# V in eight aligned blocks with key windows copied by DMA, a merged table multiply and a split last row block, in an attention and state space kernel

## The chip, the cores and the metric

The kernel runs on one core of a Trainium2 chip. The metric is the device time of one execution in microseconds (us), and the time before is the median of 11 runs. The core has TensorE (PE, matrix products into PSUM), VectorE (DVE), ScalarE (ACT), GpSimd (POOL) and SyncE (SP), which here issues nearly all transfers. They run side by side and meet through semaphores. PSUM is used as four units of two banks; a bank holds 512 float32 columns.

## The reference, cut to what matters

Two heads of work on inputs of 2048 positions and 448 features, side by side in the output. The first is attention in 16 heads of 28 over 8 keys at distances 0, 2, ..., 14. The second is a complex diagonal recurrence (state space) with real input and output.

```python
# A: sliding dilated attention
qkv = (x @ wqkv).reshape(B, S, 3, H, Dh)          # S=2048, H=16, Dh=28
idx = pos[:, None] - arange(8) * 2                # keys of a query
logits = einsum("bhsd,bhswd->bhsw", q, kg) * Dh ** -0.5   # masked where idx < 0
a = einsum("bhsw,bhswd->bhsd", softmax(logits), vg) @ wo
# B: state space
Bu = x @ B_bar.T                                  # complex, 448 states
h = Lam_bar * h + Bu[:, t]                        # for t in 0..2047
y = 2 * (hseq @ Cmat.T).real + x * Dskip
out = concatenate([a, y], -1)
```

## The kernel before, in words

Even and odd positions stand side by side, so that 2048 positions become 1024 pairs; keys at even distances are then neighbours. x comes in transposed by DMA (`xA` for attention, `xB` for the recurrence).

Attention goes over nine query blocks b. A block has 112 query pairs (the first 128) and 128 key pairs, from `k0(b)` = 112b on; neighbouring key blocks overlap by 16. V is made for each of the nine key blocks: `v{b}` on TensorE (14 matmuls in pairs of row halves, through `pair`, with a handshake by GpSimd, `tick`, in the middle), `ev{b}` evicts it to `Vt`. Each head has 29 columns there, the last one a one (`g_one`), which makes the sum of the softmax. Q and K come in column chunks 0 to 256, 256 to 512 and 512 to 1024 (`q0`, `q1`, `q2` in RANK). Their weights are spread out into `Wpad` in four quarters (`wp`), each by ScalarE or VectorE. For block b and parity: scores `s` (mask product L702, key product L706), exponentials `x` on ScalarE (L712) into one of three buffers `Pb`, the product with V `a{b}` (32 matmuls, L724), the division `n{b}` on VectorE (L730, L731), and a transposing DMA `ot{b}` into `OT`. Last, `w{t}` multiplies by `wo`.

The recurrence works in two halves of 512 pairs and four state groups k, of which k = 3 is half as large. `b` is the input product (L764, with `WT`, which seven transposing DMAs `wtx` make from `l1`, `l2`), `be` its eviction to `u`. VectorE then rotates by a table of cosines and sines (`ma`: L777, L778 or L780, L781; `ri`: L788, L789), scans (`sc`, L798), and rotates back (`mb`, then `ro`, L806, L807) into h. The table is made by `t0`, `tk`, `ts`, `t2`, `t3`, `t4` on ScalarE and VectorE. C comes in by transposing DMAs (`ctl`), and `cg`, `ch` make the scaled matrices C1 and C2 of it on VectorE (L841) after ScalarE or VectorE has scaled one part (`wtmp`). `g` makes `Gm` from C1. For each of eight row blocks t, `y{t}` is the even part (L962 with C2, L964 with Gm) and `z{t}` the odd part (L971 with C1, L974 and L976 with a diagonal for the skip, which for t = 4 to 6 VectorE adds from `xd` instead). Row block 7 evicts its odd part in two halves of 224 columns, one on ScalarE and one on VectorE, and stores it in one DMA.

The order on each engine is not the order in the source. Each step is a node with a cost, dependencies and a rank (`RANK`: start and slope over the index of a group). `Plan.run` walks a clock for each engine and takes the ready node of lowest rank; evictions that free a PSUM unit go first, and the emitted order follows. On the chip each engine runs its list in order, whatever the clock of the plan said. Rings limit how far things run ahead: `mm` four PSUM units, `P` three, `O` three, `u` three, `wt` two, `ab`, `rv`, `rs` one.

```python
n0, n1 = halves(f"v{b}", 0.188, pe, [vw], ("v", b), h, at_x(k0(b) + 128))
vn[b] = node(f"ev{b}", ab(2 * D), ev, [n1], ("v", b), frees=[(n0, 0)])
n3 = node(f"a{b}", {"P": 0.93}, pv, xs + [vn[b]] + g_1 + g_z, ("a", b), alloc="mm", frees=[(xs[0], 0), (xs[2], 0)])
```

Of the kernel before, what the change touches and what calls it, by code (L numbers as in the profile page):

```python
# [16 lines left out]
NB = 9  # L17
# [8 lines left out]

RANK = {"v": (-247.7, 33.131), "q0": (-32.25, 20.848), "q1": (-1351, 261.899), "s": (-328.09, 66.43), "a": (312.95, 100.698), "b0": (348.52, -7.748),
        "b1": (2537.88, -155.645), "d0": (308.87, 213.856), "d1": (1776.4, -98.058), "l": (1991.99, 151.071), "t": (810.76, -33.643), "tk": (305.69, 160.366),
        "xd": (2014.82, -97.299), "cg": (910.27, 8.203), "ch": (1106.04, 1.621), "g": (869.44, 168.173), "y": (701.29, 136.506), "w": (1120.33, 1.167),
        "gu": (1198.03, -204.258), "q2": (787.17, -9.125), "wp": (320.49, 73.04)}  # L30

# [185 lines left out]
def kernel(  # L217
# [24 lines left out]
    def t_(shape, dt, name, tag=None):  # L242
        return sb.tile(shape, dt, tag=tag or name, name=name)
# [16 lines left out]
    Qt = t_([128, 4, 2, NP], BF16, "Qt")  # L260
    Vt = t_([128, 2, NB, H, 29], BF16, "Vt")
    Pb = [t_([128, 4, 4, 128], BF16, f"P{i}") for i in range(3)]
# [26 lines left out]
    ACT.dma_start(Wraw[0:64, 3, :], A_wqkv[384:448, 0:2 * D])  # L289
    for i, vec in ((0, B_log_dt), (2, B_Lambda_im), (3, B_Dskip)):  # L290
        G.dma_start(rows[7 * i:7 * i + 7, :], vec.rearrange("(c p) -> c p", p=64))
    for i in range(1, 4):
        xbar_x(xA, xA2, 128 * i, 128 * i + 128)
    ACT.dma_start(rows[7:14, :], B_Lambda_re.rearrange("(c p) -> c p", p=64))
    ACT.dma_start(Wraw[:, 0:3, D:2 * D], wmain(1))
# [10 lines left out]
    SP.dma_start(Pt[64:128, :], B_B_re[384:448, :])  # L306
    xbar_x(xB, xB2, 0, 256)
    xbar_x(xB, xB2, 256, 512)

# [33 lines left out]
    def g_one(e, a):  # L343
        G.memset(Vt[:, a, :, :, 28:29].rearrange("p b h o -> p (b h) o"), 1.0)

# [194 lines left out]

    plan = Plan({"mm": 4, "P": 3, "O": 3, "wt": 2, "u": 3, "rv": 1, "rs": 1, "ab": 1})
    lazy = {}
# [107 lines left out]
    vn = {}  # L650
    for b in range(NB):
        h = {}

        def pe(part, b=b, h=h):
            if part == 0:
                h["ps"] = unit()
            pair(h, part, h["ps"], D, lambda o, k: xA[o:o + 64, k, k0(b):k0(b) + 128], lambda o, k: Wv[o:o + 64, k, :])

        def ev(e, b=b, h=h):
            evac(e, Vt[:, :, b, :, 0:28], h["ps"][:, :, 0:D].rearrange("p a (h d) -> p a h d", h=H))  # L660
        n0, n1 = halves(f"v{b}", 0.188, pe, [vw], ("v", b), h, at_x(k0(b) + 128))
        vn[b] = node(f"ev{b}", ab(2 * D), ev, [n1], ("v", b), frees=[(n0, 0)])
    qn = {}
    CH = ((0, 256), (256, 512), (512, 1024))
# [22 lines left out]
    for b in range(NB):  # L687
# [32 lines left out]
        def pv(e, b=b, h=h, hb_=hb_):  # L720
            av = h["av"] = unit()
            for par in range(2):
                for hd in range(H):
                    PE.matmul(av[:, par, 29 * hd:29 * hd + 29], hb_[par]["P"][:, hd // 4, hd % 4, :], Vt[:, par, b, hd, :], start=True, stop=True)  # L724

        def nm(e, b=b, n=n, h=h):
# [5 lines left out]
                            rc.unsqueeze(3).to_broadcast((n, 2, H, DH)), ALU.mult)  # L732
        n3 = node(f"a{b}", {"P": 0.93}, pv, xs + [vn[b]] + g_1 + g_z, ("a", b), alloc="mm", frees=[(xs[0], 0), (xs[2], 0)])
        n4 = node(f"n{b}", {"V": 1.42}, nm, [n3, g_r], ("a", b), alloc="O", frees=[(n3, 0)])
# [19 lines left out]
    for hf in range(2):  # L754
        for k in range(4):
# [15 lines left out]
            def mul(e, src, k=k, h=h, big=big):  # L771
                c, s = tab[:, 0, k, :], tab[:, 1, k, :]
                a = h["a"] = wk.tile([128, 2, HALF], BF16, tag="ra", name="ra", bufs=1)
                x = h[src]
                if big:
                    b = h["b"] = wk.tile([128, 2, HALF], BF16, tag="rb", name="rb", bufs=1)
                    V.tensor_tensor(a[:], x[:], c.unsqueeze(1).to_broadcast((128, 2, HALF)), ALU.mult)  # L777
                    V.tensor_tensor(b[:], x[:], s.unsqueeze(1).to_broadcast((128, 2, HALF)), ALU.mult)  # L778
                else:
                    V.tensor_tensor(a[:, 0], x[:, 0], c, ALU.mult)  # L780
                    V.tensor_tensor(a[:, 1], x[:, 0], s, ALU.mult)  # L781

            def ri(e, k=k, h=h, big=big):
                a = h["a"]
                v = h["v"] = wk.tile([128, 2, HALF], BF16, tag="rv", name="rv", bufs=1)
                if big:
                    b = h["b"]
                    V.tensor_tensor(v[:, 0], a[:, 0], b[:, 1], ALU.add)  # L788
                    V.tensor_tensor(v[:, 1], a[:, 1], b[:, 0], ALU.subtract)  # L789
                else:  # L790
                    V.tensor_tensor(v[0:64, 0], a[0:64, 0], a[64:128, 1], ALU.add)
                    V.tensor_tensor(v[64:128, 0], a[64:128, 0], a[0:64, 1], ALU.subtract)

# [7 lines left out]
            def ro(e, k=k, hf=hf, h=h, big=big):  # L801
                hb, a = hbuf(hf), h["a"]
                to = slice(1, HALF + 1)
                if big:
                    b = h["b"]
                    V.tensor_tensor(hb[:, k, to], a[:, 0], b[:, 1], ALU.subtract)  # L806
                    V.tensor_tensor(hb[:, k + 4, to], a[:, 1], b[:, 0], ALU.add)  # L807
                    if hf == 0:
                        V.tensor_copy(ini[:, k:k + 5:4], hb[:, k:k + 5:4, HALF])
                else:  # L810
                    V.tensor_tensor(hb[0:64, 3, to], a[0:64, 0], a[64:128, 1], ALU.subtract)
                    V.tensor_tensor(hb[64:128, 3, to], a[64:128, 0], a[0:64, 1], ALU.add)
                    if hf == 0:
                        V.tensor_copy(ini[:, 3:4], hb[:, 3, HALF:HALF + 1])
# [3 lines left out]
            n2 = node(f"be{hf}{k}", ab(1024 if big else 512), ev, [n1], rb_, alloc="u", frees=[(n1, 0)])  # L818
            m1_ = node(f"ma{hf}{k}", {"V": 1.25 if big else 0.8}, lambda e, mul=mul: mul(e, "u"), [n2, t4], rd_(0), alloc="ab", frees=[(n2, 0)])
            x = ri_ = node(f"ri{hf}{k}", {"V": 0.75 if big else 0.86}, ri, [m1_], rd_(-0.1), alloc="rv", frees=[(m1_, 0)])  # L820
            for i in range(2 if big else 1):
                x = node(f"sc{hf}{k}{i}", {"V": 1.18}, lambda e, i=i, sc=sc: sc(e, i), [x] + ([rout[0, k]] if hf else []), rd_(-0.2),
                         alloc="rs" if i == 0 else None, frees=[(ri_, 0)] if i == (1 if big else 0) else [])
                if i == 0:
                    s0 = x
            m2_ = node(f"mb{hf}{k}", {"V": 1.25 if big else 0.8}, lambda e, mul=mul: mul(e, "s"), [x, t4], rd_(-0.3), alloc="ab", frees=[(s0, 0)])
            free_ = list(wp.values()) if hf == 0 else qdone + vdone + [rout[0, j] for j in range(4)]
# [123 lines left out]
    for t in range(8):  # L951
# [14 lines left out]
        def pe1(e, t=t, tk=tk, h=h, hf=hf):  # L966
            if t == 7:
                h[1] = unit()
            ps, hb, lo = h[1], hbuf(hf), 128 * (t % 4)
            for m in range(7):  # L970
                PE.matmul(ps[:, 1, 0:D], hb[:, m, lo + 1:lo + 129], lazy["C1"][:, m, :], start=(m == 0), stop=(t in YD and m == 6), skip_group_check=True)  # L971
            if t in YD:
                return
            PE.matmul(ps[:, 1, 0:64], xB[:, 3, tk], dgO[:, 0, 0:64], start=False, stop=False, skip_group_check=True)  # L974
            for k in range(3):
                PE.matmul(ps[:, 1, 64 + 128 * k:192 + 128 * k], xB[:, 4 + k, tk], dgO[:, 1 + k, :], start=False, stop=(k == 2), skip_group_check=True)  # L976

        def ev(e, a, b, h=h):
# [8 lines left out]
        n0 = node(f"y{t}", {"P": 2.0}, pe0, hs + c2 + gn + (wdone if t > 4 else []), r, alloc="mm")  # L987
        n1 = node(f"z{t}", {"P": 1.35 if t in YD else 1.57}, pe1, [n0] + c1, (r[0], r[1], -0.1), alloc="mm" if t == 7 else None)
        if t == 7:
            g2["deps"].append(n1)  # L990
        if t < YD[0]:
# [8 lines left out]
        else:  # L1000
            def half(e, lo, hi, h=h):
                evac(e, h["o"][:, 1, lo:hi], h[1][:, 1, lo:hi])
            n2 = node(f"ye{t}0", ab(D), lambda e, ev=ev: ev(e, 0, 1), [n0] + qdone, r, frees=[(n0, 0)])
            node(f"yo{t}0", {"S": 0.6}, lambda e, st=st: st(e, 0, 1), [n2], 60 + 3 * t, lat=2.2)
            n3 = [node(f"ye{t}{1 + i}", {"AV"[i]: 0.3}, lambda e, i=i, half=half: half(e, 224 * i, 224 * i + 224), [n1, n2], r, frees=[(n1, 0)])
                  for i in range(2)]
            node(f"yo{t}1", {"S": 0.5}, lambda e, st=st: st(e, 1, 2), n3, 61 + 3 * t, lat=2.2)

# [39 lines left out]
```

## Time and profile before

| what | value |
|---|---|
| median of 11 runs | 137.59 us |
| lowest, highest | 137.15, 140.05 us |
| the profiled execution | 137.28 us, of which the span is 135.6 |
| TensorE busy | 127.9 us, 94% of the span |
| VectorE busy | 109.8 us, 81% |
| ScalarE busy | 89.7 us, 66% |
| GpSimd busy | 29.0 us, 21% |
| V products, L528 and L529 | 63 matmuls each, about 350 ns each, in pairs |
| rotations, 1024 columns (L777, L778) | 24 operations, 682 to 690 ns |
| DMA | 15.59 MB, mean 115 GB/s |

The profile is of one execution. The span runs from the first to the last recorded event; the execution's own time is a little longer. Busy times overlap, so their sum is no time. Matmuls are pipelined: one is longer in the record than the step from its start to the next one's, so steps are read from starts. Idle time in a row is that of its engine just before it, with what ended it. The line numbers L are those of the kernel before.

### The profile page before, as it was taken

The numbers are of one execution on the slowest core, as the hardware profiler recorded it, in microseconds if no ns is written. First come the engines' busy times: TensorE is split into PE (matmuls) and PEld (weight loads), VectorE is DVE, ScalarE is ACT, GpSimd is POOL, SyncE is SP. The second block draws the span as 40 slices with busy tenths as digits, with TensorE's granted clock in tenths as the row PEclk, the third lists the DMA queues.
The fourth block names the chain that finished last, engine by engine and source line by source line (L and its number), as shares of the span: only waits on it lengthen the run. The fifth ranks groups of instructions, "written<-read, shape, count | busy, mean of one in ns | idle before, by whom it ended". The sixth has DMA issues, their size and how long they took to land.

```text
span 135.6 us, 3784 instructions
## 1 busy us (share of the span) xinstructions
PE 127.9 (94%) x1525; PEld 70.0 (52%) x1530; DVE 109.8 (81%) x204; ACT 89.7 (66%) x122; POOL 29.0 (21%) x110
## 2 busy tenths in 40 slices
PE   6989999999989999999999999999999999999980
PEld 2334757787434554564544465654665655455540
DVE  0438999999989899999999999999999999911110
ACT  0039999979995966999967998754875237511120
POOL 6985154013899500000000000000000000000000
PEclk9999999999999999999999999999999999999999
DMA  3999998509679587133020008741134788442121
GB/s 90 249 323 247 261 196 149 73 2 111 119 150 194 115 169 140 35 64 59 0 45 19 0 0 64 181 120 68 63 71 118 169 88 277 151 135 73 68 102 44
DMA packets 42755, 15.59 MB, mean 115 GB/s; under 512 B 34927, under 2 KB 42735, under 8 KB 42735
## 3 DMA queue, kind: packets, MB, share of 16 engines
q1 hardware_dynamic: 41264, 14.11, 49.7%
q10 hardware_dynamic: 1374, 1.21, 3.0%
q8 instruction: 13, 0.21, 0.7%
q14 instruction: 8, 0.06, 0.2%
q0 software_dynamic: 96, 0.00, 0.1%
HBM read 3.62 MB, written 3.67 MB: 54 GB/s over the span
## 4 chain that ended last, share of the span: by engine, by line
PE 74%; ACT 15%; POOL 5%; issue 2%; DVE 0%; POOLq 0%; ACTq 0%
PE mm L528 22%; PE mm L764 14%; PE mm L962 8%; PE mm L971 8%; PE mm L724 6%; PE mm L964 4%; PE mm L861 4%; PE mm L702 4%; PE mm L706 3%; ACT Wpad L501 2%; ACT Wpad L500 2%; POOL mst L312 2%; ACT tab L454 1%; ACT P L712 1%; ACT Wpad L497 1%
## 5 line engine op out<-in xcount | busy, mean ns | idle before, releaser
L712 ACT ACTIVATE P<-mm 128x896 bf16<-128x896 f32 (+1 forms) x36 | 31.5, 933 | 4.9 <-PE mm L706 4.9
L528 PE MATMUL mm<-xA,Wpad 64*128 64x256 bf16 (+1 forms) x168 | 27.0, 305 | 0.3 <-DVE Qt L507 0.3
L529 PE MATMUL mm<-xA,Wpad 64*128 64x256 bf16 (+1 forms) x168 | 26.8, 305 | 0.1
L505 ACT CAST ys<-mm 128x896 bf16<-128x896 f32 (+2 forms) x15 | 11.4, 771 | 19.1 <-PE mm L971 8.9
L536 POOL MEMSET tick<- 1x1 f32 x41 | 4.9, 119 | 84.9 <-PE mm L529 84.7
L764 PE MATMUL mm<-xB,WT 128*128 128x512 bf16 x93 | 22.2, 379 | 0.6 <-ACT P L712 0.3
L528 PEld LDWEIGHTS <-Wpad 64*128 64x128 bf16 x168 | 15.0, 94 | 7.4 <-POOL tick L536 0.6
L529 PEld LDWEIGHTS <-Wpad 64*128 64x128 bf16 x168 | 14.8, 94 | 1.6 <-issue 0.8
L764 PEld LDWEIGHTS <-WT 128*128 128x128 bf16 x98 | 9.0, 98 | 11.2 <-issue 1.1
L528 PE MATMUL mm<-Wv,xA 64*128 64x448 bf16 x63 | 13.7, 349 | 1.1 <-POOL tick L536 0.6
L529 PE MATMUL mm<-Wv,xA 64*128 64x448 bf16 x63 | 13.7, 350 | 0.0
L971 PE MATMUL mm<-C,h 128*128 128x448 bf16 x56 | 11.9, 353 | 0.0
L962 PE MATMUL mm<-C,h 128*128 128x448 bf16 x56 | 11.9, 353 | 0.0
L528 PE MATMUL mm<-wo,OT 64*128 64x448 bf16 x56 | 10.8, 349 | 0.0
L529 PE MATMUL mm<-wo,OT 64*128 64x448 bf16 x56 | 10.8, 349 | 0.0
L731 DVE TENSOR_TENSOR O<-mm,rcs 112x896 bf16<-112x896 f32 (+1 forms) x9 | 9.8, 1091 | 0.3
L528 PEld LDWEIGHTS <-xA 64*128 64x128 bf16 x63 | 5.5, 94 | 6.5 <-POOL tick L536 1.8
L996 DVE TENSOR_TENSOR ys<-mm,xd 128x448 bf16<-128x448 f32 x3 | 1.9, 625 | 8.5 <-ACT ys L505 8.5
L507 DVE CAST Vt<-mm 128x896 bf16<-128x896 f32 x6 | 6.4, 1086 | 2.9 <-PE mm L529 2.9
L724 PE MATMUL mm<-Vt,P 128*128 128x29 bf16 x288 | 8.7, 176 | 0.0
L798 DVE TENSOR_TENSOR_SCAN rs<-p_r,ini,rv 128x512 bf16<-128x512 f32 x7 | 8.6, 1270 | 0.0
L798 DVE TENSOR_TENSOR_SCAN rs<-p_r,rv 128x512 bf16<-128x512 f32 x7 | 8.5, 1221 | 0.0
(175 smaller groups left out, 247.3 us busy)
## 6 DMA issues: line engine op xcount, KB each, us to landing
out_dram<-ys SPq DMA_DIRECT2D x15, 224.0 KB, 2.4
Wraw<-in_A_wqkv_dram ACTq DMA_DIRECT2D x2, 336.0 KB, 4.0
wo<-in_A_wo_dram SPq DMA_DIRECT2D x2, 336.0 KB, 3.3
Wv<-in_A_wqkv_dram ACTq DMA_DIRECT2D x1, 336.0 KB, 3.5
natW<-in_B_B_re_dram SPq DMA_DIRECT2D x1, 336.0 KB
natW<-in_B_B_im_dram SPq DMA_DIRECT2D x1, 336.0 KB, 5.0
xo<-in_B_x_dram SPq DMA_DIRECT2D x1, 336.0 KB
out_dram<-ys SPq DMA_DIRECT2D x2, 112.0 KB, 1.7
```

Of the source, the lines that this page charges most:

```text
L505: ACT.copy(o, i)
L507: V.tensor_copy(o, i)
L528: x = PE.matmul(ps[:, a, 0:n], lhs(0, lo[i]), rhs(0, lo[i]), start=(i == 0), stop=(i == 6), skip_group_check=True)
L529: y = PE.matmul(ps[:, b, 0:n], lhs(64, hi[i]), rhs(64, hi[i]), start=(i == 0), stop=(i == 6), skip_group_check=True)
L702: PE.matmul(at(g)[:, 0:4 * n].rearrange("p (s q) -> p s q", s=4), msk[32 * g:32 * g + 32, 0, :], msk[32 * g:32 * g + 32, 1:2, c0:c0 + n].t ...
L712: ACT.activation(P[:].rearrange("p s g q -> p g s q")[:, 2 * z:2 * z + 2, :, 0:n], h["s"][z][:, :, 0:4 * n].rearrange("p g (s q) -> p g s ...
L724: PE.matmul(av[:, par, 29 * hd:29 * hd + 29], hb_[par]["P"][:, hd // 4, hd % 4, :], Vt[:, par, b, hd, :], start=True, stop=True)
L731: V.tensor_tensor(O[0:n, :].rearrange("p (a h d) -> p a h d", a=2, h=H), avv[0:n, :, :, 0:DH], rc.unsqueeze(3).to_broadcast((n, 2, H, DH)) ...
L764: PE.matmul(ps[:, i, :], WT[:, j, 128 * m:128 * m + 128], xB[:, j, HALF * hf:HALF * hf + HALF], start=(j == 0), stop=(j == 6))
L798: V.tensor_tensor_scan(h["s"][:, i], p["r2"][:, k:k + 1].to_broadcast((128, HALF)), h["v"][:, i], 0.0 if hf == 0 else ini[:, m:m + 1], ALU ...
L962: PE.matmul(ps[:, 0, 0:D], hb[:, m, lo:lo + 128], lazy["C2"][:, m, :], start=(m == 0), stop=False, skip_group_check=True)
L971: PE.matmul(ps[:, 1, 0:D], hb[:, m, lo + 1:lo + 129], lazy["C1"][:, m, :], start=(m == 0), stop=(t in YD and m == 6), skip_group_check=True)
```

## The change

V is made in eight aligned blocks of 128 key pairs (`Va`). Key blocks 0 and 8 are V blocks 0 and 7 as they are. For key blocks 1 to 7 two DMAs inside SBUF, issued by SyncE (`vi{b}`), copy the last 16b rows of V block b - 1 and the first 128 - 16b rows of block b to a window `vw`, of which there is one buffer. `a{b}` waits for its window and frees it.

The two table multiplies of a rotation become one over twice the columns, with both operands broadcast. In row block 7 the odd part is made in two pieces of 320 and 128 columns, each in its own PSUM unit, evicted by VectorE and ScalarE and stored by a DMA each. The vector Lambda_re comes through GpSimd's queue rather than ScalarE's, and the first half of `xB` in four transposes of 128 rather than two of 256. All ranks of the plan are other numbers, so the order on each engine changes too.

```diff
-RANK = {"v": (-247.7, 33.131), "q0": (-32.25, 20.848), "q1": (-1351, 261.899), "s": (-328.09, 66.43), "a": (312.95, 100.698), "b0": (348.52, -7.748),
-        "b1": (2537.88, -155.645), "d0": (308.87, 213.856), "d1": (1776.4, -98.058), "l": (1991.99, 151.071), "t": (810.76, -33.643), "tk": (305.69, 160.366),
-        "xd": (2014.82, -97.299), "cg": (910.27, 8.203), "ch": (1106.04, 1.621), "g": (869.44, 168.173), "y": (701.29, 136.506), "w": (1120.33, 1.167),
-        "gu": (1198.03, -204.258), "q2": (787.17, -9.125), "wp": (320.49, 73.04)}
+RANK = {"vi": (-263.4, 62.011), "v": (-254.81, 47.21), "q0": (-9.3, 24.721), "q1": (-1234.39, 223.716), "s": (-87.89, 63.579), "a": (69.32, 137.31),
+        "b0": (401.81, -35.09), "b1": (2710.84, -237.429), "d0": (173.54, 248.333), "d1": (1637.27, -116.832), "l": (2365.77, 124.008), "t": (604.07, -43.7),
+        "tk": (493.73, 94.516), "xd": (2163.8, -62.364), "cg": (762.25, 41.377), "ch": (1274.79, -39.858), "g": (616.28, 111.784), "y": (692.93, 168.195),
+        "w": (1273.74, 32.648), "gu": (1290.91, -260.374), "q2": (564.28, 20.748), "wp": (192.19, 111.406)}
-    Vt = t_([128, 2, NB, H, 29], BF16, "Vt")
+    Va = t_([128, 8, 2, H, 29], BF16, "Va")
-    for i, vec in ((0, B_log_dt), (2, B_Lambda_im), (3, B_Dskip)):
+    for i, vec in ((0, B_log_dt), (1, B_Lambda_re), (2, B_Lambda_im), (3, B_Dskip)):
         G.dma_start(rows[7 * i:7 * i + 7, :], vec.rearrange("(c p) -> c p", p=64))
-    ACT.dma_start(rows[7:14, :], B_Lambda_re.rearrange("(c p) -> c p", p=64))
-    xbar_x(xB, xB2, 0, 256)
-    xbar_x(xB, xB2, 256, 512)
+    for i in range(4):
+        xbar_x(xB, xB2, 128 * i, 128 * i + 128)
-        G.memset(Vt[:, a, :, :, 28:29].rearrange("p b h o -> p (b h) o"), 1.0)
+        G.memset(Va[:, 4 * a:4 * a + 4, :, :, 28:29].rearrange("p b a h o -> p (b a h) o"), 1.0)
-    plan = Plan({"mm": 4, "P": 3, "O": 3, "wt": 2, "u": 3, "rv": 1, "rs": 1, "ab": 1})
+    plan = Plan({"mm": 4, "P": 3, "O": 3, "wt": 2, "u": 3, "rv": 1, "rs": 1, "ab": 1, "vw": 1})
-    for b in range(NB):
+    for b in range(8):
...
-            pair(h, part, h["ps"], D, lambda o, k: xA[o:o + 64, k, k0(b):k0(b) + 128], lambda o, k: Wv[o:o + 64, k, :])
+            pair(h, part, h["ps"], D, lambda o, k: xA[o:o + 64, k, 128 * b:128 * b + 128], lambda o, k: Wv[o:o + 64, k, :])
...
+    vw_ = {0: (None, vn[0]), 8: (None, vn[7])}
+    for b in range(1, NB - 1):
+        h = {}
+
+        def win(e, b=b, h=h):
+            h["w"] = wk.tile([128, 2, H, 29], BF16, tag="vw", name="vw", bufs=1)
+            SP.dma_start(h["w"][0:16 * b], Va[128 - 16 * b:128, b - 1])
+            SP.dma_start(h["w"][16 * b:128], Va[0:128 - 16 * b, b])
+        vw_[b] = h, node(f"vi{b}", {"S": 1.1}, win, [vn[b - 1], vn[b]] + g_1, ("vi", b), alloc="vw", lat=2.1)
...
-        n3 = node(f"a{b}", {"P": 0.93}, pv, xs + [vn[b]] + g_1 + g_z, ("a", b), alloc="mm", frees=[(xs[0], 0), (xs[2], 0)])
+        n3 = node(f"a{b}", {"P": 0.93}, pv, xs + [vw_[b][1]] + g_1 + g_z, ("a", b), alloc="mm",
+                  frees=[(xs[0], 0), (xs[2], 0)] + ([(vw_[b][1], 0)] if 0 < b < NB - 1 else []))
...
-                    V.tensor_tensor(a[:], x[:], c.unsqueeze(1).to_broadcast((128, 2, HALF)), ALU.mult)
-                    V.tensor_tensor(b[:], x[:], s.unsqueeze(1).to_broadcast((128, 2, HALF)), ALU.mult)
+                    V.tensor_tensor(a[:], x[:].unsqueeze(1).to_broadcast((128, 2, 2, HALF)), tab[:, :, k, :].unsqueeze(2).to_broadcast((128, 2, 2, HALF)), ALU.mult)
                 else:
-                    V.tensor_tensor(a[:, 0], x[:, 0], c, ALU.mult)
-                    V.tensor_tensor(a[:, 1], x[:, 0], s, ALU.mult)
+                    V.tensor_tensor(a[:, 0], x[:, 0:1].to_broadcast((128, 2, HALF)), tab[:, :, k, :], ALU.mult)
...
+        def piece(e, lo, n, ds, tk=tk, h=h):
+            ps, hb = unit(), hbuf(1)
+            h["z", lo] = ps
+            for m in range(7):
+                PE.matmul(ps[:, 1, 0:n], hb[:, m, 385:513], lazy["C1"][:, m, lo:lo + n], start=(m == 0), stop=False, skip_group_check=True)
+            for k in ds:
+                a, b = (0, 64) if k == 0 else (128 * k - 64, 128 * k + 64)
+                PE.matmul(ps[:, 1, a - lo:b - lo], xB[:, 3 + k, tk], dgO[:, k, 0:b - a], start=False, stop=(k == ds[-1]), skip_group_check=True)
...
-            n3 = [node(f"ye{t}{1 + i}", {"AV"[i]: 0.3}, lambda e, i=i, half=half: half(e, 224 * i, 224 * i + 224), [n1, n2], r, frees=[(n1, 0)])
-                  for i in range(2)]
-            node(f"yo{t}1", {"S": 0.5}, lambda e, st=st: st(e, 1, 2), n3, 61 + 3 * t, lat=2.2)
+            for i, (lo, n, ds) in enumerate(((0, 320, (0, 1, 2)), (320, 128, (3,)))):
+                n0 = n1 = node(f"z{t}{i}", {"P": (1.15, 0.52)[i]}, lambda e, lo=lo, n=n, ds=ds, piece=piece: piece(e, lo, n, ds),
+                               [n0] + c1, (r[0], r[1], -0.1), alloc="mm")
+                n3 = node(f"ye{t}{1 + i}", {"VA"[i]: (0.42, 0.2)[i]}, lambda e, lo=lo, n=n, h=h: evac(e, h["o"][:, 1, lo:lo + n], h["z", lo][:, 1, 0:n]),
+                          [n1, n2], r, frees=[(n1, 0)])
+                node(f"yo{t}{1 + i}", {"S": 0.5}, lambda e, lo=lo, n=n, tk=tk, h=h: SP.dma_start(outv[tk, 1, D + lo:D + lo + n], h["o"][:, 1, lo:lo + n]),
+                     [n3], 61 + i + 3 * t, lat=2.2)
+            g2["deps"].append(n1)
```

## The prediction

> **What bounds the kernel now.** I read the page first, then the busy time by stage, then the chain of waits, and last the rows of TensorE, VectorE and the DMA queue around the places that the change touches. From the page, the slices of the span and the head of the chain that ended last:
>
> ```profile
> PE   6989999999989999999999999999999999999980
> DVE  0438999999989899999999999999999999911110
> ACT  0039999979995966999967998754875237511120
> PEclk9999999999999999999999999999999999999999
> PE 74%; ACT 15%; POOL 5%; issue 2%; DVE 0%; POOLq 0%; ACTq 0%
> ```
>
> TensorE is busy in every slice from the third to the last but one, at full clock. But VectorE is as full until slice 34. The stages show how close the two are (sum of busy time, instructions in brackets):
>
> ```profile
> 20.00:34.00 14.00, 13.51 (x213) 10.62 (x209) 13.52 (x24) 13.16 (x22) 3.84 (x19) 1.00 0.59 85
> 40.00:87.00 47.00, 46.58 (x624) 24.04 (x628) 45.20 (x79) 38.81 (x51) 6.68 (x21) 1.00 0.40 76
> 87.00:117.40 30.40, 30.40 (x396) 17.06 (x394) 29.70 (x50) 17.82 (x22) 0.70 (x8) 1.00 0.54 126
> 117.40:131.40 14.00, 14.00 (x79) 7.30 (x77) 2.96 (x4) 2.65 (x5) 0.00 (x0) 1.00 0.29 97
> ```
>
> The columns after the length are PE, weight loads, VectorE, ScalarE, GpSimd. From 40 to 117.4 us TensorE has 76.98 of 77.4 us, VectorE 74.90. From 117.4 us TensorE is alone: y rows 4 to 7. So a gain needs less work on both engines up to 117.4 us, and less TensorE work or a shorter tail after it.
>
> Two rows decide how far TensorE may run ahead, the last C2 products on VectorE and the first y product, which needs all of them (chain of waits):
>
> ```profile
> 83.02 1.27 DVE L841 SCALAR_TENSOR_TENSOR C<-CT,p_sh,wtmp 128x448 bf16<-128x448 bf16 x2
> 86.95 1.33 PE mm L962 x7
> ```
>
> C2 is done at 84.29, y0 starts at 86.95: slack 2.66 us. Likewise the last write of h (L807) ends at 115.67 and y4, which needs it, starts at 117.43: slack 1.76 us. The tail, all three rows from the timeline:
>
> ```profile
> 131.46 0.35 ACT L505 CAST ys<-mm 128x224 bf16<-128x224 f32 x1 [0.94 <-PE mm L976]
> 131.83 0.39 DVE L507 CAST ys<-mm 128x224 bf16<-128x224 f32 x1 [2.75 <-ACT ys L505]
> 132.25 0.34 SPq L984 DMA_DIRECT2D out_dram<-ys  x1
> ```
>
> VectorE takes its half only when ScalarE has finished: the halves lie in one PSUM bank and are read in turn. From the last issue to the end of the span is 135.6 - 132.25 = 3.35 us.
>
> **The change, part by part.** The sum is made against the profiled execution: 137.28 us, of which 135.6 is span. The median shown is 137.59, 0.31 above it.
>
> V in eight blocks. Fourteen matmuls go. They run in pairs on two row halves, a pair every 0.19 us (9.36, 9.56, 9.75 in the timeline): 7 x 0.19 = 1.32 us off TensorE, and one eviction of 896 columns (0.91 us on ScalarE or 1.09 on VectorE).
>
> Order. The ranks are new, so the emitted order was compared. Before the first exponentials TensorE gets one 512-column K/Q block more (7 x 0.2157 = 1.51 us), after them one fewer. VectorE evicts three V blocks early instead of six but builds two Wpad quarters instead of one (2.0 us). ScalarE builds two instead of three (3.0 us less), with two V blocks (1.7) and a 512-column K block (0.9) more and one 256-column block (0.5) fewer. Net ScalarE -0.9; but the cosine table waits for the tables' earlier passes, so I move the first exponential from 38.22 only to about 37.9. The first b product ends, as now, near 38.7 (-1.32 + 1.51, less lost waits), and the rotations start on VectorE at 40.1 as before.
>
> One table multiply. Two 1024-wide products start 0.61 apart and the next, dependent, operation 0.71 later: 1.32 us. The row for 1024 elements is 0.69 long, that for 512 is 0.42, so 512 elements are 0.27 and 2048 take 0.69 + 0.54 = 1.23, with the gap 1.25. That saves 0.07 in twelve places, and by the same reckoning 0.075 in four small ones: 1.14 us. The old product already read a broadcast operand, so I expect the same rate. Bounds: a gain of 1.5, or, if the doubly broadcast form ran at half rate, +1.07 on each big one, +13 us. I take the near row.
>
> VectorE's balance. From the first rotation to the last C2: a Q block +1.15, u of 1024 instead of 512 columns +0.55, one scale more +0.48, one pair of additions moved ahead +0.88, Gm gone to ScalarE -1.01, multiplies -0.65: +1.40, less the 0.42 us that VectorE now waits for a0. C2 is done at 84.29 + 1.4 - 0.2 = 85.5 (half the wait counted). To the last h: +1.15 + 0.55 + 0.48 - 1.01, two xd products moved ahead +1.12, one y eviction moved behind -0.99, multiplies -1.14: +0.16, so 115.5 to 115.8.
>
> TensorE's balance. y0 could start at 86.95 - 0.3 (earlier exponentials) - 1.51 + 0.5 (one score step now ahead of y0) = 85.6, so C2 and TensorE arrive together. One score step fewer follows: y4 at 117.43 - 1.35 - 0.5 = 115.6, and h is done by 115.8. I take y4 at 115.75: gain 1.68.
>
> Windows. Seven windows, each two SP issues of about 0.55 and 128 rows of 1856 bytes, 238 KB. One buffer serves them, so a window is issued only when the previous product a has read it. Time from that release to use: 0.1 + 1.1 + landing. A plain copy inside SBUF is not in the trace; the nearest row is the 224 KB store, landing 1.7 / 2.4 / 3.5 (min, median, max), and a transpose out of O lands in 2.8 to 4.3. Bounds 2.9 and 5.5 us, I take 3.6. TensorE's work between uses, from the chain's pieces: a3 to a4 (two score steps, one b product) 4.1; a6 to a7 (y2, z2, a score step) 4.25; a2 to a3 5.8; the other gaps are over 9. Window 2 waits for the C transposes on SP instead (to about 56.9 + 1.1 + 2.4 = 60.4) and a2 comes at 61.4. So 0.5 us or more is left everywhere: cost 0, at most 1.4 in a4 and 1.25 in a7.
>
> Queues. SP: x of B in four pieces, 4 x 1.36 against 3.71, is 1.7 later, window 1 puts 1.1 in front of Ctn and WT; the first WT issue moves from 24.07 to about 24.3, while its pair's operand comes 4 us earlier. Later windows stand ahead of the transposes of O, of wo (86 us, used at 106) and of y stores, all with many us in hand. The queue waits in a window for TensorE, and what stands behind it is these same transposes. GpSimd: one issue more, 0.52, shifts pad, eye and masks; the last row vector lands near 7.7 and its transpose runs at 8.85. Zero for these; at most 0.5 if that transpose waits. ScalarE loses a 0.79 us issue, before its first work.
>
> Last odd rows. Pieces of 320 and 128 columns stream the same 448, with seven more weight loads behind them and one more start: +0.07. After TensorE's end T, ScalarE's 128 columns take 0.27 (0.35 for 224, 0.53 for 448) from T + 0.11. VectorE's 320 columns take 0.49 and are done at T + 0.14, since that piece ends 0.45 before T; its store is issued from T + 0.17 for 0.53, so the last issue starts at T + 0.72, not T + 0.90: -0.18. SP's own issue is what is late next. The last store shrinks from 112 to 32 KB; from 1.7 us for 112 KB and 2.4 for 224, that is worth up to -0.5. Against it stands the Trainium skill, "DMA: Bandwidth & Descriptors", Specifications: runs below 512 bytes are read, modified and written, and these runs are 256 bytes. Counted twice for that, as 64 KB, the same slope leaves -0.3 (an estimate from that page's rule). By the row the tail gains 0.7, by the rule 0.5; I count 0.2, because the row's slope below 112 KB is not shown, and keep 0 and -0.7.
>
> Sum: -1.68 + 0.07 - 0.18 = -1.79. Own execution 135.5, median 135.8.
>
> **The rivals.** (1) The gain is partly lost between two full engines: TensorE and VectorE now arrive together at y0 and y4, so each small wait of either counts. For it: 2.66 and 1.76 us of slack go. Against it: the waits of VectorE after 40 us are under 1 us now. If half of them repeat on each side the gain is 0.4 to 1.1: 136.5 to 137.2.
> (2) Slower: the window wait. If release to use takes 5.7 us, a4 stands 1.6 and a7 1.45, y0 having no slack left: -1.79 + 3.05 = +1.26, 138.9. It decides from about 5.1 us on. For it: the slowest transposes; against: the page's DMA slices from 54 to 81 us read 1 3 3 0 2 0 0 0, so nothing stands in a window's way there.
> (3) The merged multiply doesn't keep its rate: +13 on a chain that ends together with TensorE's, about 148. Against it: the 1024-wide row with a broadcast has the rate already.
> (4) The early stage gains too: if ScalarE's 0.9 us reach the exponentials and the store its slope, -2.7: 134.9.
>
> **How the numbers follow.** Main case 0.55 (135.2 to 136.4). Rival 1 0.24, of which a half faster, the rest within the bound or a little above; rival 2 0.12; rival 3 0.04; rival 4 0.05. A measurement of this kernel can tell 0.3%, 0.4 us, from no change. Faster 0.55 + 0.05 + 0.12 = 0.72, same 0.08, slower 0.20. The range leaves out rival 3, most of rival 2 and a few in a hundred below: 134.9 to 137.7.
>
> **What would show it.** Right: y4's first product near 115.7 us, V matmuls 112 instead of 126, merged multiplies near 1.23 us, window landings near 2.4 us with no TensorE wait before an a product, last store issued 0.7 us after TensorE's end. Wrong: TensorE idle before a4 or a7 released by a DMA, VectorE later than 116 us at the last h, or the early stage ending after 40.2 us.

## The result, and the profile after

Against the kernel before, the changed kernel takes 0.9904 of the time, with an interval of 0.9877 to 0.9931: 1.3 us less, where 1.79 was predicted. Two repetitions gave 0.991 (0.9888 to 0.9932) and 0.9893 (0.9842 to 0.9944), medians 136.41 us of 22 executions and 136.13 of 6. The ratios leave out the executions of the changed kernel from 137.6 us on; of the first ten these are six, with a mean granted clock of 0.975 to 0.986, so that the median of those ten, 138.12, stands above the 137.64 of the kernel before.

The profile below is from the first repetition (137.24 us, span 135.5); it is one of the slower executions of that series, 0.8 us above its median. First the page's slices and the head of the chain that ended last:

```profile
PE   6649999999989999999999899999999999999980
DVE  0606999999899799999999999999999999811130
PEclk9999999999999999999999999999999999999999
PE 69%; ACT 10%; DMA 8%; DVE 6%; issue 3%; SPq 1%; ACTq 0%
```

What is new stands at the front: slices two and three show TensorE at 6 and 4 tenths where the kernel before had 9 and 8, VectorE drops to 0 in the third, and the chain now holds 8% of DMA. Then the stages behind the start of the rotations, with the bounds at the same places of the schedule as in the profile before (PE, weight loads, VectorE, ScalarE, GpSimd; then clock, DMA share and GB/s):

```profile
41.30:87.60 46.30, 45.44 (x633) 23.86 (x633) 44.50 (x69) 38.52 (x51) 6.29 (x19) 1.00 0.42 88
87.60:117.60 30.00, 30.00 (x382) 16.87 (x378) 28.90 (x44) 17.30 (x21) 0.71 (x8) 1.00 0.66 157
117.60:131.60 14.00, 14.00 (x86) 7.67 (x84) 3.34 (x5) 2.65 (x5) 0.00 (x0) 1.00 0.29 97
```

TensorE is still the full engine, with 45.44 of 46.30 us in the first of these stages and all of the other two. The two places where VectorE could stop it, in the timeline: the last C2 product and y0, the last write of h and y4.

```profile
86.08 0.68 DVE L848 SCALAR_TENSOR_TENSOR C<-CT,p_sh,wtmp 128x448 bf16<-128x448 bf16 x1
87.59 0.73 PE L969 MATMUL mm<-C,h 128*128 128x448 bf16 x3
...
116.23 0.42 DVE L814 TENSOR_TENSOR h<-ra 128x512 bf16<-128x512 bf16 x1
117.63 0.55 PE L969 MATMUL mm<-C,h 128*128 128x448 bf16 x2
```

VectorE is 0.83 us early at y0 and 0.98 at y4 (2.66 and 1.76 before). The merged multiplies, in the groups by shape (busy time, mean ns), and the tail in the timeline:

```profile
L788 DVE TENSOR_TENSOR ra<-u,tab 128x2048 bf16<-128x2048 bf16 x6 | 7.3, 1224 | 0.1
```

```profile
131.23 0.49 DVE L506 CAST ys<-mm 128x320 bf16<-128x320 f32 x1 [1.94 <-PE mm L990]
131.68 0.27 ACT L504 CAST ys<-mm 128x128 bf16<-128x128 f32 x1 [0.96 <-PE mm L990]
131.75 0.82 SPq L1021 DMA_DIRECT2D out_dram<-ys  x2
```

The two evictions no longer follow one another. But y4 comes at 117.63, later than before (117.43), although TensorE has less to do. The time is lost before the first exponentials. Early rows of the timeline, before and after:

```profile
4.31 0.40 ACTq L295 DMA_DIRECT2D Wraw<-in_A_wqkv_dram  x1
7.39 0.38 ACTq L298 DMA_DIRECT2D Wraw<-in_A_wqkv_dram  x1
7.42 0.36 PE L528 MATMUL mm<-Wv,xA 64*128 64x448 bf16 x1 [0.25 <-DMA xA<-in_A_x_dram]
8.85 0.20 PE L392 MATMUL mm<-eye,rows 28*64 28x28 bf16 x1
...
38.22 1.94 ACT L712 ACTIVATE P<-mm 128x1024 bf16<-128x1024 f32 x2
```

```profile
2.52 0.61 ACTq L294 DMA_DIRECT2D Wraw<-in_A_wqkv_dram  x1
6.92 0.37 ACTq L297 DMA_DIRECT2D Wraw<-in_A_wqkv_dram  x1
9.54 0.36 PE L527 MATMUL mm<-Wv,xA 64*128 64x448 bf16 x1 [1.67 <-DMA xA<-in_A_x_dram]
10.97 0.20 PE L391 MATMUL mm<-eye,rows 28*64 28x28 bf16 x1
...
39.53 1.02 ACT L723 ACTIVATE P<-mm 128x1024 bf16<-128x1024 f32 x1
```

The K weights (the second `Wraw` load) are issued at 2.52 us, not 4.31. TensorE waits for x of A: its second V block starts at 9.54, not 7.42. Behind that block, in TensorE's order, stands the transposition of the row vectors, at 10.97 and not 8.85; all tables come from it, and the first exponentials, behind the tables, run at 39.53 and not 38.22. From there to the last ScalarE eviction it is 92.15 us, against 93.24 before. So a gain of 1.09 us is there, behind a later start.

Why the load starts earlier is seen in the emitted list of ScalarE's queue. In these programs the transfers of the SP and ScalarE queues take eight completion counters in turn, and an issue waits for the counter's last user, the transfer eight before. Before, the K weights were the ninth transfer (first line) and waited for the V weights, which landed at 4.3 us: the VectorE copy that waits for them starts at 4.32. With the Lambda_re row gone to GpSimd's queue they are the seventh and wait for nothing (second line):

```
L295 DMACopy Wraw<-in_A_wqkv_dram 128x3x448 [waits DMAHW0_49]
L294 DMACopy Wraw<-in_A_wqkv_dram 128x3x448
```

The load behind it, of the Q weights, shifts as well. Before, it waited for the second transpose of x and was issued at 7.39 us; now it waits for the first one and is issued at 6.92, while TensorE still waits for the second. All runs below that move the K weights move this load too, so the share of each in the delay is not shown.

### The profile page after: what moved, and what is told of

The parts are those of the page before. It is cut to its first block, busy times and chain, and to the rows that moved or that the text cites. A ratio compares the mean times of both kernels' runs of the same rounds, so it can differ in the third digit from the quotient of the medians.

```text
span 136.7 us, 3782 instructions
## 1 busy us (share of the span) xinstructions
PE 127.7 (93%) x1518; PEld 71.0 (52%) x1523; DVE 108.3 (79%) x191; ACT 88.1 (64%) x118; POOL 29.0 (21%) x110
## 4 chain that ended last, share of the span: by engine, by line
PE 72%; ACT 11%; DMA 5%; DVE 5%; issue 3%; SPq 1%; ACTq 0%
PE mm L527 21%; PE mm L777 14%; PE mm L969 8%; PE mm L976 7%; DMA xA<-in_A_x_dram 5%; PE mm L736 5%; PE mm L971 4%; PE mm L868 4%; PE mm L713 3%; PE mm L717 2%; ACT P L723 2%; ACT wtmp L510 2%; ACT Kt L504 1%; ACT tab L453 1%; PE mm L528 1%
## 5 line engine op out<-in xcount | busy, mean ns | idle before, releaser
L527 PE MATMUL mm<-xA,Wpad 64*128 64x256 bf16 (+1 forms) x168 | 26.4, 305 | 0.2 <-ACT Va L504 0.2
L504 ACT CAST ys<-mm 128x896 bf16<-128x896 f32 (+2 forms) x16 | 12.1, 774 | 22.4 <-PE mm L976 8.9
L528 PE MATMUL mm<-xA,Wpad 64*128 64x256 bf16 (+1 forms) x168 | 26.4, 305 | 0.0
L527 PEld LDWEIGHTS <-Wpad 64*128 64x128 bf16 x168 | 15.3, 94 | 7.0 <-POOL tick L535 0.2
L528 PEld LDWEIGHTS <-Wpad 64*128 64x128 bf16 x168 | 15.0, 94 | 0.8 <-issue 0.6
L969 PE MATMUL mm<-C,h 128*128 128x448 bf16 x56 | 11.9, 353 | 0.0
L976 PE MATMUL mm<-C,h 128*128 128x448 bf16 x49 | 10.4, 353 | 0.0
L736 PEld LDWEIGHTS <-P 128*128 128x128 bf16 x288 | 8.1, 96 | 1.3 <-issue 0.4
L504 ACT CAST u<-mm 128x1024 bf16<-128x1024 f32 (+1 forms) x6 | 5.2, 870 | 4.7 <-PE mm L777 4.5
```

Of the source, the lines that this page charges most:

```text
L504: ACT.copy(o, i)
L527: x = PE.matmul(ps[:, a, 0:n], lhs(0, lo[i]), rhs(0, lo[i]), start=(i == 0), stop=(i == 6), skip_group_check=True)
L528: y = PE.matmul(ps[:, b, 0:n], lhs(64, hi[i]), rhs(64, hi[i]), start=(i == 0), stop=(i == 6), skip_group_check=True)
L969: PE.matmul(ps[:, 0, 0:D], hb[:, m, lo:lo + 128], lazy["C2"][:, m, :], start=(m == 0), stop=False, skip_group_check=True)
```

## The experiments

All kernels here keep the order of the other instructions on every engine, so that a difference is that of the edit. Ratios are to the kernel before, with their intervals.

**The changed kernel again.** No edit.

> The changed kernel once more, to have its profile and its ratio beside the variants on the same chip. Theory (as predicted): against the kernel before 0.987 to 0.993, that is 135.9 to 136.6 us; from the second b product (L777) to the first product of y4 (L969) 75.8 us against 77.2 before, and from the end of TensorE to the end of the span some 0.3 us less than the 4.25 of before. Rival (the gain is in the early stage and not in TensorE's work): the stretch from b01 to y4 is as long as before, and b01 comes earlier than 38.7 us.

Measured: 0.991 (0.9888 to 0.9932), in the slower half of what was expected. The stretch from the second b product to y4 was 76.1 us (41.52 to 117.63), 0.4 of which is a wait for a window shown further on. The rival falls: the second b product came later than before, not earlier.

**The Lambda_re row back on ScalarE's queue.**

```diff
-    for i, vec in ((0, B_log_dt), (1, B_Lambda_re), (2, B_Lambda_im), (3, B_Dskip)):
+    for i, vec in ((0, B_log_dt), (2, B_Lambda_im), (3, B_Dskip)):
...
+    ACT.dma_start(rows[7:14, :], B_Lambda_re.rearrange("(c p) -> c p", p=64))
     ACT.dma_start(Wraw[:, 0:3, D:2 * D], wmain(1))
```

> The changed kernel with one queue edit undone: the Lambda_re row is again loaded from ScalarE's queue, between the last V weights and the K weights, and not from GpSimd's. Theory A (the prediction: that issue costs nothing on either queue): the same time as the changed kernel, within 0.3%. Theory B (with the 0.79 us issue gone, the big K and Q weight loads start 1 to 2 us earlier and run against the transposes of x of A, which TensorE waits for at 8 to 12 us): the waits of TensorE on xA shrink by 0.5 us or more and the kernel is 0.3 to 0.8 us faster, 0.984 to 0.988 of the kernel before. Rival C: the last row vector comes later from the slower queue, the tables later, and the time grows by up to 0.8 us.

Measured: 135.88 us, 0.9883 (0.9844 to 0.9922). In its profile (135.5 us, span 133.8) the K weights are issued at 4.42 us, the row vectors are transposed at 9.02 and the first exponentials run at 37.92. Here are these rows and the two places in its timeline:

```profile
4.42 0.40 ACTq L295 DMA_DIRECT2D Wraw<-in_A_wqkv_dram  x1
...
9.02 0.20 PE L392 MATMUL mm<-eye,rows 28*64 28x28 bf16 x1
...
37.92 2.85 ACT L724 ACTIVATE P<-mm 128x1024 bf16<-128x1024 f32 x3
...
84.44 0.69 DVE L849 SCALAR_TENSOR_TENSOR C<-CT,p_sh,wtmp 128x448 bf16<-128x448 bf16 x1
85.53 1.48 PE L970 MATMUL mm<-C,h 128*128 128x448 bf16 x7
...
114.36 0.42 DVE L815 TENSOR_TENSOR h<-ra 128x512 bf16<-128x512 bf16 x1
115.61 0.55 PE L970 MATMUL mm<-C,h 128*128 128x448 bf16 x2
```

y0 was predicted at 85.6 and y4 at 115.75. With this one edit undone the predicted schedule appears, and the execution, the quickest of its six, is 1.78 us below that of before (137.28); the medians differ by 1.7. That is what theory B has, but the interval overlaps that of the changed kernel, so the next three runs ask for the mechanism.

**A spare load in the old place.** Lambda_re stays on GpSimd's queue; a load that nothing reads goes ahead of the K weights.

```diff
+    spare = t_([7, 64], BF16, "spare")
+    ACT.dma_start(spare[:, :], B_Lambda_re.rearrange("(c p) -> c p", p=64))
     ACT.dma_start(Wraw[:, 0:3, D:2 * D], wmain(1))
```

> The changed kernel, Lambda_re still loaded from GpSimd's queue, with one small load more at its old place on ScalarE's queue (the same 7x64 row into a spare tile that nothing reads), so that the K weights are again the fifth issue of that queue. Theory (it is the early start of the K weights that costs, not GpSimd's fourth load): the K weights are issued at 4.3 to 4.5 us and not at 2.5, TensorE's transposition of the row vectors (L392) runs near 9.0 us and not at 9.6 to 12.2, and the time is that of the kernel with Lambda_re on ScalarE's queue, 135.9 us, 0.4 to 0.5 us below the changed kernel. Rival (GpSimd's extra load is what comes late): the row transposition stays late and the time stays at 136.4.

Measured: 135.91 us, 0.9869 (0.9836 to 0.9902), all six executions between 135.84 and 136.27. From its timeline:

```profile
4.12 0.45 ACTq L296 DMA_DIRECT2D Wraw<-in_A_wqkv_dram  x1
7.80 0.36 PE L529 MATMUL mm<-Wv,xA 64*128 64x448 bf16 x1 [0.31 <-DMA xA<-in_A_x_dram]
9.23 0.20 PE L393 MATMUL mm<-eye,rows 28*64 28x28 bf16 x1
```

A load more makes the kernel quicker by the medians. GpSimd's fourth load, which is still there, is not what comes late; what matters is when the K weights start, and the Q weights with them.

**The queue edit alone, in the kernel before.** Lambda_re goes from ScalarE's queue to GpSimd's, with nothing else changed.

> The kernel before with only the queue of the Lambda_re row changed, from ScalarE's to GpSimd's, all else in the same order. Theory (the early K weights delay the transposes of x of A, whatever comes later): the row transposition moves from 8.85 us to 9.6 or later in most executions, the first exponentials from 38.2 by the same amount, and the median is 0.4 to 1.0 us above the kernel before, with a wider spread. Rival (the cost appears only with eight V blocks, whose second block needs the second transpose sooner): within 0.2 us of the kernel before.

Measured: 139.88 us, 1.0092 (1.0031 to 1.0153). One small load moved between queues makes the kernel before slower by about 1%, more than was expected, so the loss does not need the eight V blocks. But much of it goes with a lower clock: in four of the six executions the mean granted clock is 0.969 to 0.988 (in one of eleven of the kernel before on the same chip), and the other two, 138.08 and 138.30 us, are only 0.4 us above the 137.8 that the kernel before takes at full clock. The profiled execution was the quickest of the six, with the row vectors at 9.38 us (8.85 before) and the exponentials at 38.83.

**Two spare loads.** The K weights then wait for the second transpose.

```diff
+    spare = t_([7, 2, 64], BF16, "spare")
+    for i in range(2):
+        ACT.dma_start(spare[:, i, :], B_Lambda_re.rearrange("(c p) -> c p", p=64))
     ACT.dma_start(Wraw[:, 0:3, D:2 * D], wmain(1))
```

> The changed kernel with two small spare loads on ScalarE's queue ahead of the K weights and not one (nothing reads them), so that the K weights wait for the second transpose of x of A and are issued near 7.6 us. Theory (what counts is what runs beside the transposes of x): the row vectors are transposed near 8.9 us, not later than with one spare load; but the K weights land near 12 us, where ScalarE wants them at 11.2 to 11.5, so the time is 135.7 to 136.4, no better than with one (135.9). Rival (the later the better, without limit): another 0.3 us or more off, 135.5. Rival (the spare loads themselves disturb): above 136.5.

> The changed kernel again, as the partner of the one with two spare loads on the same chip. Theory: 0.990 to 0.992 of the kernel before, 136.2 to 136.5 us, with the row vectors transposed at 9.6 us or later. Rival (the gap to the kernels with late K weights came from the chips): the same time as its partner within 0.1 us.

Measured: 136.69 us, 0.9917 (0.9889 to 0.9945) with two, 136.13 us, 0.9893 (0.9842 to 0.9944) for the changed kernel. The row vectors came at 9.19, as with one spare load and not before it. ScalarE then had to wait for the weights, in the timeline of the kernel with two spare loads:

```profile
7.58 0.40 ACTq L297 DMA_DIRECT2D Wraw<-in_A_wqkv_dram  x1
...
12.39 0.75 ACT L499 COPY Wpad<-Wraw 128x672 bf16<-128x672 bf16 x1 [0.82 <-DMA Wraw<-in_A_wqkv_dram]
```

So the load has a best time: at 2.5 us it delays x, at 7.6 it is late itself, by somewhat more than was expected, and 4.1 to 4.4 is between. On this chip the changed kernel was the quicker of the two by 0.56 us, against the rival of its repetition. Over the executions that the ratios count, the median is 136.27 for its two repetitions (24), and 135.89 for the two kernels with the load at 4.1 to 4.4 (11); these come in part from different chips, and the intervals of all these ratios overlap.

**More TensorE work in the early stage.**

```diff
-            pair(h, part, h["ps"], D, lambda o, k: xA[o:o + 64, k, 128 * b:128 * b + 128], lambda o, k: Wv[o:o + 64, k, :])
+            for _ in range(2 if part == 0 and b in (6, 7) else 1):
+                pair(h, part, h["ps"], D, lambda o, k: xA[o:o + 64, k, 128 * b:128 * b + 128], lambda o, k: Wv[o:o + 64, k, :])
```

> The changed kernel with 16 matmuls more in the early stage: in V blocks 6 and 7 the first four pairs are run twice, the second time overwriting the first; everything else in the same order. Eight pairs at 0.188 us are 1.50 us of TensorE work, a little more than the 1.32 that the eight blocks took away. Theory A (early TensorE work counts in full): 1.4 to 1.6 us slower than the changed kernel, about the time of the kernel before. Rival B (the first exponentials, which ScalarE and the cosine table set, decide when the stage ends, and TensorE has slack ahead of them): under 0.7 us slower.

Measured: 1.0061 (1.0034 to 1.0088), median 138.29: 1.9 us above the changed kernel's 136.41 on the same chip. At a mean granted clock above 0.99 alone it is 137.93 (13 executions) against 136.32 (19), 1.6 us. From the row vectors' transposition (10.22) to the first exponentials (40.45) it is 30.23 us, against 28.56: 1.67 more for 1.50 of work. Early TensorE work counts in full, and so should the 1.32 us of the V block. The rival falls.

**Two multiplies again.**

```diff
-                    V.tensor_tensor(a[:], x[:].unsqueeze(1).to_broadcast((128, 2, 2, HALF)), tab[:, :, k, :].unsqueeze(2).to_broadcast((128, 2, 2, HALF)), ALU.mult)
+                    V.tensor_tensor(a[:, 0], x[:], tab[:, 0:1, k, :].to_broadcast((128, 2, HALF)), ALU.mult)
+                    V.tensor_tensor(a[:, 1], x[:], tab[:, 1:2, k, :].to_broadcast((128, 2, HALF)), ALU.mult)
```

(and the small one likewise)

> The changed kernel with each table multiply as two instructions again, 16 more on VectorE, in the same order on all engines. Theory A (VectorE has 0.6 us in hand at the last C2 and 0.9 us at the last write of h, as the profile of the changed kernel shows): the 1.14 us that the single multiply saves reach TensorE only in part, 0.3 to 0.6 us slower than the changed kernel. Rival B (VectorE is the limiter): 1.1 us slower. Rival C (VectorE's work is hidden altogether, so the merged multiply brought nothing): within 0.2 us of the changed kernel. Rows: a pair of 1024-wide multiplies 1.32 us from the first start to the dependent operation, against 1.24 for the single one.

Measured: 136.39 us, 0.9911 (0.9875 to 0.9947), the time of the changed kernel; theory A and rival B fall, rival C stands. The two places in its timeline:

```profile
85.31 0.69 DVE L850 SCALAR_TENSOR_TENSOR C<-CT,p_sh,wtmp 128x448 bf16<-128x448 bf16 x1
86.14 1.11 PE L971 MATMUL mm<-C,h 128*128 128x448 bf16 x5
...
115.69 0.42 DVE L816 TENSOR_TENSOR h<-ra 128x512 bf16<-128x512 bf16 x1
116.18 1.12 PE L971 MATMUL mm<-C,h 128*128 128x448 bf16 x5
```

VectorE is now done 0.14 us before y0 and 0.07 before y4. From the first exponentials (38.37) to y4 it is 77.81 us, with Lambda_re back on ScalarE's queue 77.69 (37.92 to 115.61). The merged multiply only widens VectorE's slack, from 0.14 and 0.07 us here to 0.40 and 0.83 in the kernel with Lambda_re back.

**The merged multiply alone, in the kernel before.** The multiplies, `ri` and `ro` of the changed kernel in the kernel before.

> The kernel before with only the table multiplies merged, 16 instructions fewer on VectorE, all else in the same order. Theory (VectorE has 2.66 us in hand at the last C2 and 1.76 at the last write of h, so its gain is only more slack): the last write of h comes 0.8 to 1.1 us earlier, and the time is that of the kernel before within 0.2 us. Rival (each shortened wait of TensorE counts somewhere on the way): 0.3 to 0.8 us faster.

Measured: 0.9991 (0.9963 to 1.002), as the theory has it. The last write of h ended at 115.30 instead of 115.67, less than the 0.8 to 1.1 us expected.

**Windows in six pieces.**

```diff
-            SP.dma_start(h["w"][0:16 * b], Va[128 - 16 * b:128, b - 1])
+            n = 16 * b
+            for lo, hi in ((0, n // 4), (n // 4, n // 2), (n // 2, n)):
+                SP.dma_start(h["w"][lo:hi], Va[128 - n + lo:128 - n + hi, b - 1])
...
```

(the second piece likewise)

> The changed kernel with each window copied in six pieces of rows and not two: the same bytes in four more issues on the SP queue, about 2.3 us from the first issue to the last. Theory (windows have little in hand; from the release to the use there are 4.0 us before a4 and 4.1 before a7, and six issues take 3.4 and the landing 2.0 to 2.9): TensorE waits 1.5 to 2.2 us before a4 and as much before a7, and 0.4 to 1.0 before a2, whose window waits for the C transposes: 3.5 to 5 us slower than the changed kernel, 139.9 to 141.4. Rival (the copies of windows are hidden with much to spare): under 0.5 us slower.

Measured: 146.97 us, 1.0654 (1.0602 to 1.0705): 10.6 us above the changed kernel, over twice what was expected. The waits of TensorE from 60 to 112 us, the window of a7 in the timeline, and two stages around it:

```profile
PE mm L740 <- DMA vw<-Va: 4.3, 3, 2.1
...
PE mm L740 <- ACT P L727: 2.4, 1, 2.4
```

```profile
102.61 2.54 SPq L670 DMA_DIRECT2D vw<-Va  x3
105.19 1.95 SPq L673 DMA_DIRECT2D vw<-Va  x3
...
108.59 0.96 PE L740 MATMUL mm<-vw,P 128*128 128x29 bf16 x32 [2.13 <-DMA vw<-Va]
```

```profile
106.00:110.00 4.00, 1.87 (x59) 1.43 (x58) 1.55 (x3) 1.46 (x2) 0.00 (x0) 1.00 0.37 82
110.00:114.00 4.00, 4.00 (x27) 1.76 (x22) 3.49 (x3) 1.73 (x2) 0.00 (x0) 0.57 0.80 209
```

Six issues took 4.5 us, not 3.4. TensorE waited 4.3 us for windows and 2.4 for exponentials that came late behind a3. After each wait over 2 us its clock fell: 0.57 from 110 to 114 us, behind the wait of 2.13, and 0.62 from 80 to 84, behind the one of 2.4 for exponentials. The mean granted clock is 0.974 over 145.1 us against 0.996 over 135.5, which is 3.2 us more lost. Together 9.9 us, or 9.5 without the 0.4 that the changed kernel waits for a window itself, and the spans differ by 9.6. So the windows have little in hand: the rival falls. The changed kernel itself shows the edge. In its profile one issue takes 1.91 us instead of 0.55 (timeline, the window of a4):

```profile
70.92 0.51 SPq L668 DMA_DIRECT2D vw<-Va  x1
71.52 1.91 SPq L669 DMA_DIRECT2D vw<-Va  x1
...
75.41 0.96 PE L736 MATMUL mm<-vw,P 128*128 128x29 bf16 x32 [0.40 <-DMA vw<-Va]
```

From the release (70.89, the end of a3) to the use it is 4.5 us here, and a4 waits 0.40. What held that issue stays open. Three other profiles with the K weights as the seventh transfer have one window issue of 1.4 to 1.7 us, without a wait behind it, and the first profile of the changed kernel has none; the four with Lambda_re or spare loads on ScalarE's queue have none above 0.6.

**The split of the last odd rows alone, in the kernel before.** `piece`, two evictions and two stores as in the changed kernel.

> The kernel before with only the last odd rows of y made in 320 and 128 columns in two PSUM banks. From the predicted steps: 0.07 us more on TensorE, the last store issued 0.6 to 0.7 us after TensorE's end and not 0.9, so 0.1 to 0.3 us faster than the kernel before (0.998 to 0.999). If the slope of the store rows held down to 32 KB: 0.6 faster. If the 256-byte runs of the last store cost more than the earlier issue saves: 0 to 0.3 slower.

Measured: 137.65 us, 0.9998 (0.9957 to 1.0038): no difference that the measurement can tell. In its profile (span 135.6, as before) the last rows are:

```profile
131.47 0.27 ACT L505 CAST ys<-mm 128x128 bf16<-128x128 f32 x1 [0.96 <-PE mm L983]
131.55 0.82 SPq L1014 DMA_DIRECT2D out_dram<-ys  x2
```

The last issue is over at 132.37, against 132.59 before, and the last store takes 1.5 us to land and not 1.7; but the span ends at 135.6 in both.

**A version meant to beat both.** Lambda_re on ScalarE's queue, and the last store issued there as well.

```diff
-SP.dma_start(outv[tk, 1, D + lo:D + lo + n], h["o"][:, 1, lo:lo + n])
+(ACT if lo else SP).dma_start(outv[tk, 1, D + lo:D + lo + n], h["o"][:, 1, lo:lo + n])
```

> A version meant to beat both: the changed kernel with Lambda_re loaded from ScalarE's queue again, and the last 128-column store issued from ScalarE's queue, right behind the copy that makes it, and not from SP behind the 320-column store. Theory: the early stage as in the two runs with the K weights issued at 4.3 us, 135.9 us; the last issue begins at T + 0.4 and not T + 0.65, so 0.1 to 0.3 us less: 135.6 to 135.8, 0.985 to 0.987 of the kernel before. Rival: the end of the span does not follow the last issue (the split of the last rows alone brought nothing), 135.9.

Measured: 136.03 us, 0.9865 (0.9822 to 0.9907). It beats the kernel before, and cannot be told from the two kernels above with the K weights at 4.1 to 4.4 us; the store's queue brought nothing that shows. In its profile (136.1 us) the K weights went out at 4.16, but TensorE still waited 1.55 us for x and the row vectors came at 10.02: so the later issue does not exclude a late transpose. Of the four profiles with the weights issued at 4.1 us or later this is the only one with the row vectors after 9.3.

## Why the prediction was right, and where it was not

The case that carried the forecast is the one that happened, 0.5 us short. Its arithmetic on TensorE holds; one step on the queues failed. By its steps:

- *V in eight blocks, 1.32 us off TensorE.* Shown from the other side: 1.50 us put back cost 1.7 us in the profile and 1.6 to 1.9 in the medians.
- *Order: the first exponentials at about 37.9, the rotations at 40.1.* 37.92 and 39.51 with Lambda_re back on ScalarE's queue; 39.53 and 41.11 in the changed kernel as it is. The order was read rightly, its start was not. No run has the eight blocks with the old ranks, or `xB` in two transposes again, so what these are worth by themselves is not shown.
- *Queues: "ScalarE loses a 0.79 us issue, before its first work. Zero for these".* This is the step that failed. The issue's own length was weighed, and what stood behind it was not: a 336 KB load that came forward by 1.8 us (and a second one by 0.5) and ran beside the transposes of x, for which TensorE waits first. It cost 0.4 us by the medians (136.27 against 135.89), 1.3 us in the profile above. The half microsecond kept for a late row-vector transposition was the right place with the wrong cause: not its load, but TensorE's order, held up by x.
- *Merged multiply 1.23 us.* 1.22 to 1.25 measured. Its worth for the time was taken as part of VectorE's balance and never by itself; by itself it is none in the kernel before and under 0.2 us here.
- *C2 done at 85.5 and y0 at 85.6; h by 115.8 and y4 at 115.75.* With the queue undone 85.13, 85.53, 114.78 and 115.61. TensorE leads both, so rival 1, small waits between two full engines, did not come; it would have had little room, 0.40 us at y0.
- *Windows: 3.6 us taken, 4.1 and 4.25 to be had, decisive from about 5.1.* The place was right and the room too: 4.5 us from release to use cost 0.40 in one execution, six issues cost 10.6 us. The windows landed in 1.9 to 4.1 us in that profile, median 2.9, where 2.4 was the sign of being right. The price in rival 2 was too low, since the clock's fall after a stall was not in it.
- *Last odd rows: 0.18 to the good.* The eviction and the issue moved as worked out, by 0.2 us; the end of the span did not follow in the kernel before. Of the predicted sum this term is not shown. (From the last ScalarE eviction to the end it is 4.14 us before, and 3.82 to 4.17 in the profiles with the split: the end moves by 0.3 us for a reason that no run here tells.) The weighing of row against rule can't be decided either: the last landing took 1.5 us for 32 KB and 1.7 for 112 KB, and nothing of that shows in the end.
- *Rival 4, an early stage that gains more*, turned round: the early stage lost.

The sum of the kernel with Lambda_re back on ScalarE's queue: first exponentials 0.30 us earlier, from there to the last ScalarE eviction 91.74 against 93.24, the rest 4.14 in both. That is 1.80, for a predicted 1.79, but the agreement to 0.01 is luck: the 0.18 predicted at the tail did not come, TensorE's stretch gave as much more, and this is one execution, the quickest of six.

## What to carry to other kernels

When an issue leaves a queue, price what moves up behind it: which transfer starts earlier, and which transfer that the first engine waits for it will run beside. A load that is wanted late should be held back on purpose, and it can have a best time; here a small load that nothing needs did it. And price a TensorE stall of about 2 us with the clock that follows it, not by its length alone.

## What the runs showed of the hardware that was not expected

TensorE's clock fell after stalls of about 2 us. In the kernel with six-piece windows a wait of 2.13 us was followed by four us at 0.57. In the first profile of the changed kernel (138.40 us) a wait of 2.05 us for x did the same:

```profile
9.53 0.47 PE L527 MATMUL mm<-Wv,xA 64*128 64x448 bf16 x1 [2.05 <-DMA xA<-in_A_x_dram]
```

```profile
9.00:14.00 5.00, 4.47 (x30) 1.80 (x32) 1.61 (x6) 0.54 (x1) 2.33 (x8) 0.66 1.18 270
9.66:13.07 3.41, 3.41 (x22) 1.21 (x20) 0.79 (x1) 0.00 (x0) 1.61 (x7) 0.50 1.21 304
```

The clock is at half from 9.66 to 13.07 us (second line), and in the six-piece kernel likewise:

```profile
110.34:113.75 3.41, 3.41 (x11) 1.32 (x9) 3.15 (x3) 1.53 (x2) 0.00 (x0) 0.50 0.76 198
```

Half of 3.41 us is 1.7 us lost each time, nearly as much as the wait. In the repetition a wait of 1.67 us at the same place left the clock at full speed. The Trainium skill, "TensorE: Matmul & The Clock Gate", Part 1: The HAM clock gate, has the clock fall to half after an idle window of about 3.4 us that runs free of the kernel. The half rate fits these rows, and so does the length of the fall, 3.41 us; but gaps of 2.05 and 2.13 us were enough here, shorter than that figure. Whether the length of a gap decides or where it falls, no run here tells.

Through such falls the earlier load can cost more than the medians above say. A mean granted clock below 0.99 is found in 10 of 38 executions of the changed kernel, in 1 of 18 of the three with the K weights at 4.1 to 4.4 us, and in 11 of 87 of the kernel before that stand beside these variants. They come from different chips, and only one such execution of the changed kernel was profiled, so that the load is the cause of the rest is not shown.
